# State products as three column tiles, a costed register read and a new table of priorities, in a chunked attention and two-layer MoE kernel

## The chip, the cores and the metric

The kernel runs on one core of a Trainium2 chip. The metric is the device time of one execution in microseconds. The kernel before takes 762.5 us, the median of three runs (762.09 to 762.78).

The core has five instruction streams that run side by side and wait for one another through semaphores: TensorE (PE; its weight loads stand apart as PEld), VectorE (DVE), ScalarE (ACT), GpSimd (POOL) and SyncE (SP, which here issues DMAs and reads registers). Each stream is executed in the order in which the program has its instructions.

## The reference

Three layers follow each other. All tensors are fp32.

```python
# 1. attention with a decaying state: 4 batches, 8 heads, 768 steps, head size 48
for t in range(S):
    S_re, S_im = a[t] * (S_re, S_im)          # complex product, per row of the state
    S_re = S_re + outer(k[t], v[t])
    y[t] = q[t] @ S_re
# 2. dense layer on x = y, [3072, 384], hidden size 2048
h = x @ w_in
x = (max(h, 0) + alpha * min(h, 0)) @ w_out
# 3. sparse layer: 8 experts of hidden size 1024, one expert per row
on = x @ w_skip > 0
e  = argmax(x @ w_gate);  gate = softmax(x @ w_gate)[e]
out = x;  out[on] += gate * (max(x @ w1[e], 0) @ w2[e])
```

## The kernel before, in words

**Attention.** The 768 steps are cut into 6 chunks of 128, and each chunk of each batch is one unit: 24 units, s = 0 to 23, with chunk c = s // 4. For a unit, DVE and ACT first work out decays, angles and scaled q and k ("E", function `elementwise`). Then the function `attention` ("P") issues on TensorE: the products of keys and queries (tile `at`, two halves of four heads), the transposes of the keys (also into `at`, copied by ACT to `kT`), the output `y`, and, except in the last chunk, the new part of the state, `sps`, which DVE adds to the state `St`. `sps` is the product of `kT` (128 steps x 96 rows per head; 96 is real and imaginary part of 48) and the values `vt` (128 steps x 48). It is 8 matmuls, one per head, each with 96 columns of weights and 48 columns that stream past them (lines 709 to 711). They are 8 separate items for the scheduler, so that other matmuls can stand between them. The output `y` is different: its matmuls have 32 columns of weights and go to four groups of 32 rows of the output, and the helper `columns` adds all of them to the plan as one item (lines 697 to 706 and 727 to 735). An fp32 matmul makes two records, since TensorE passes over it twice; one with fp32r operands makes one.

**Dense layer.** Two units of attention make one block of 256 rows: 12 blocks, "M0" to "M11" (`moe_block`). A block has 8 steps. A step makes 18 matmuls into a tile `h` (weights split in a high and a low part, input split in `xhi` and `xlo`), then ACT copies `h` to `hs`, DVE applies the leaky slope, ACT rounds to `gh`, DVE takes the rest `gl`, and 12 matmuls of the step before go into the accumulators `acc`. At the start, the dense layer's 64-bit weights are decoded on DVE ("d", `decode`).

**Sparse layer.** Rows are listed per expert by indirect DMAs. After block M9, `rank_experts` orders the experts by their count: a small matmul of `onesb` and `ohsum` counts, a chain of small DVE operations writes `plan`. Then SP reads from `plan` two registers for each of nine work items (`start_of`, lines 997 to 1005, helper lines 1002 and 1003). An item's row numbers `ids` are read from the list by a DMA on SP's queue whose address is in these registers (line 1046), and POOL gathers the rows into `xg` by indirect DMAs (line 1056). DVE takes the maximum of the gate's logits from `xg` into `gmx` (function `gates_of`), and TensorE transposes `xg` into `xt`. The weights of the item come by DMAs of SP's queue (`load_weights`, line 1014). The first item's rows are gathered while blocks M10 and M11 still run.

**The order.** All this is recorded as a plan of items, each with an engine, a cost in us, what it reads and writes, and a priority. `Plan.emit` walks through the plan with these costs as if they were times, lets each engine take the ready item with the lowest priority number, and writes the instructions out in the order that comes of it. A table `SHIFT` adds a number to the priority of an item by its label (for instance "P5s": state product of unit 5; "M3.2": step 2 of block 3). So a cost or a shift that changes changes the order of the instructions on all five streams, and nothing else. Between 27 and 55 us of the plan's own clock it fills pauses of TensorE with matmuls that nobody reads ("filler", line 1420).

Of the kernel before, what the change touches and what calls it, by code (L numbers as in the profile page):

```python
# [52 lines left out]
PE_IN, PE_OUT = [], [4, 5, 6, 7, 8, 9, 10, 11]  # L53
C0, C1 = [4, 6]
SHIFT = {
# [24 lines left out]
}  # L80
MODE = [0] * 12
TRIG = "trig_and_small"
# [316 lines left out]
def moe_kernel(tc, a, qk, v, w_in, w_out, alpha, w_gs, w1, w2, nat, nat_v, out):  # L399
# [53 lines left out]
    def mm(o, l, r, start, stop):  # L453
        n = cols(o)
        dt = l.dtype
        if dt == F32R:
            cost = max(n, 256) / 2.4 + 13.5
        elif dt == BF16:
            cost = 30
        else:  # L460
            cost = 2 * (max(n, math.prod(l.shape[1:])) / 1.2 + (6 if n <= 128 else 0))
        pl.add("PE", cost / 1e3, lambda: nc.tensor.matmul(real(o), lhsT=real(l), rhs=real(r), start=start, stop=stop,  # L462
                                                          skip_group_check=True),
               [l, r] + ([] if start else [o]), [o])
# [28 lines left out]
    with ctx:  # L493
# [172 lines left out]
        def attention(s, pri):  # L666
            c, b = divmod(s, NB)
            last = c == NCH - 1
            qh, kh = qk_of[s, 0], qk_of[s, 1]
            pl.pri = V_PRI if s < 2 else pri(0)  # L670
            pl.part = "v"
            vt = pl.buf(pp, [128, VW], F32, "vt", bufs=2)
            dma(vt, v[s], VT)
            m = s // 2
            if s % 2 == 0:
                x_of[m] = [pl.buf(xp, [128, 3, 256], F32R, name, bufs=2) for name in ("xhi", "xlo")]
            xhi, xlo = x_of[m]
            y = pbuf(y_ps, [128, 3, 128], "y")
            m4 = mask.rearrange("p (o f) -> p o f", o=1).to_broadcast([128, 4, 128])
            As, kTs = [], []  # L680
            for g in range(2):
                pl.pri, pl.part = pri(g), 'ab'[g]
                at = pbuf(at_ps, [128, 512], "at", bufs=2)
                for x in range(4):
                    mm(at[:, x * 128:(x + 1) * 128], kh[:, 4 * g + x, 0:128], qh[0:96, 4 * g + x, :], True, True)
                A = pl.buf(pp, [128, 4, 128], F32, "A", bufs=2)
                tt(A, at.rearrange("p (x t) -> p x t", x=4), m4, ALU.mult)
                As.append(A)
                if not last:
                    at = pbuf(at_ps, [128, 512], "at", bufs=2)  # L690
                    for x in range(4):
                        transpose(at[:, x * 96:x * 96 + 96], kh[:, 4 * g + x, 0:128], ident[0:96, 0:96])
                    kT = pl.buf(pp, [128, 4, 96], F32, "kT", bufs=2)
                    copy(kT, at[:, 0:384].rearrange("p (x d) -> p x d", x=4))
                    kTs.append(kT)
            pl.pri, pl.part = pri(2), 'y'
            ops = []
            for inter in range(c > 0, -1, -1):
                for g in range(2):
                    for t, off in ((g, 16 * g), (2, 32 - 48 * g)):  # L700
                        for x in range(4):
                            h = 4 * g + x
                            cs = slice(h * 64 + off, h * 64 + off + 32)
                            ops.append((y[32 * x:32 * x + 32, t, :],) + (
                                (St[:, b, cs], qh[:, h, :]) if inter else (vt[:, cs], As[g][:, x, :])))
            columns(ops)
            pl.pri, pl.part = pri(3), 's'
            if not last:
                sps = pbuf(s_ps, [128, H * D], "sps")[0:96, :]
                for h in range(H):  # L710
                    mm(sps[:, h * D:h * D + D], kTs[h // 4][:, h % 4, :], vt[:, h * 64:h * 64 + D], True, True)
                new = sps.rearrange("p (h e) -> p h e", h=H)
                sv = St[0:96, b, :].rearrange("p (h e) -> p h e", h=H)[:, :, 0:D]
                gc = kh[:, :, 128:129].to_broadcast([96, H, D])
                if c:
                    su = pl.buf(pp, [96, H, D], F32, "su", bufs=1)
                    tt(su, new, sv, ALU.add)
                    tt(sv, su, gc, ALU.mult)
                else:
                    tt(sv, new, gc, ALU.mult)  # L720
            pl.part = 'h'
            cs = slice((s % 2) * 128, (s % 2) * 128 + 128)
            copy(xhi[:, :, cs], y)
            tt(xlo[:, :, cs], y, xhi[:, :, cs], ALU.subtract)
            pl.part = ''

        def columns(ops):

            def go():
                for n, (o, l, r) in enumerate(ops):  # L730
                    ins = nc.tensor.matmul(real(o), lhsT=real(l), rhs=real(r), start=n < 4,  # L731
                                           stop=n >= len(ops) - 4, skip_group_check=True)
                return ins

            pl.add("PE", 0.3 + 0.0575 * len(ops), go, [x for op in ops for x in op[1:]], [op[0] for op in ops])

        def decode64(src, n, name):
            raw = pl.buf(dp, [128, 384, 2], I32, "raw", bufs=RAW)
# [258 lines left out]
        def start_of(n):  # L997

            r, _, col = ITEMS[n]

            def read():
                regs[n] = (nc.sync.value_load(real(plan)[0:1, r:r + 1], min_val=0, max_val=E - 1),
                           nc.sync.value_load(real(plan)[0:1, col:col + 1], min_val=0, max_val=(E - 1) * NT + 256))

            return pl.add("SP", 0.2, read, [plan], [])

        def load_weights(n, place, place1, after, behind=None):
            r1 = pl.buf(place1, [128, 3, FE], F32, "r1", bufs=1 + (place1 is in_B))
# [31 lines left out]
        def gather(n, place, k, opened, listed, rows=NT):  # L1040
# [13 lines left out]
            for t in range(nt):  # L1054
# [5 lines left out]
                    gathers[n] = r.ins  # L1060
                    return r

                pl.add("POOL", 1.1, go, [ids], [xg[:, t, :]], lag=0.7, late=1.0)
            return ids, xg

        def gates_of(place, xg, nt):
# [485 lines left out]
```

## Time and profile before

| | us |
|---|---|
| median of the runs (3) | 762.5 |
| the profiled execution | 760.46 |
| its span, from the first to the last instruction | 758.3 |
| TensorE busy | 718.6 (95%) |
| VectorE busy | 602.1 (79%) |
| ScalarE busy | 486.7 (64%) |
| GpSimd busy | 98.6 (13%) |
| mean granted clock of TensorE | 0.996 of full speed |

Busy times are of the profiled execution. A matmul's record begins when it starts and is longer than its share of the engine, since matmuls overlap: how long one occupies TensorE is read from one start to the next.

### The profile page before, as it was taken

What the parts mean: (1) busy time and instruction counts of PE and PEld (TensorE: products, weight loads), DVE (VectorE), ACT (ScalarE), POOL (GpSimd) and SP (SyncE); (2) the same over time, 40 slices, a digit from 0 to 9 for tenths busy, and PEclk for the clock granted to TensorE, in tenths of its full rate; (3) what the DMA queues carried; (4) which work ended last, traced back from release to release, by engine and by line L of the source; (5) the groups of instructions that cost most, each with busy time, mean ns of one, the idle gap of its engine ahead of it and who ended that gap; (6) DMA issues with size and microseconds to landing.
All of it is one profiled execution on the core that took longest, in us unless ns stands there. A gap on an engine that the chain in (4) does not pass through costs nothing.

```text
span 758.3 us, 16570 instructions
## 1 busy us (share of the span) xinstructions
PE 718.6 (95%) x6372; PEld 695.5 (92%) x6372; DVE 602.1 (79%) x1425; ACT 486.7 (64%) x833; POOL 98.6 (13%) x154
## 2 busy tenths in 40 slices
PE   1789999999999999999999999999997999999996
PEld 0678999999999999999999999999997999999996
DVE  5999999989889899999899898945555635697623
ACT  8969659869779679897948958522325332556411
POOL 4000000111101220011130010101011013710111
PEclk9999999999999999999999999999999999999999
DMA  7595862483744767668475564936215301899500
GB/s 267 161 273 199 239 214 79 124 257 102 189 117 143 188 175 231 183 181 268 137 195 178 180 193 120 250 108 172 87 44 189 126 1 46 274 390 393 181 11 18
DMA packets 84678, 130.53 MB, mean 172 GB/s; under 512 B 8822, under 2 KB 60096, under 8 KB 84592
## 3 DMA queue, kind: packets, MB, share of 16 engines
q1 hardware_dynamic: 79152, 111.19, 48.4%
q0 software_dynamic: 5440, 18.21, 7.6%
q8 instruction: 52, 0.85, 0.5%
q14 instruction: 34, 0.28, 0.1%
HBM read 99.46 MB, written 31.29 MB: 172 GB/s over the span
## 4 chain that ended last, share of the span: by engine, by line
PE 49%; issue 10%; DVE 7%; ACT 5%; DMA 5%; SPq 2%; POOL 1%; POOLq 0%; ACTq 0%; DVEq 0%
PE h L462 20%; PE acc L462 19%; PE at L462 3%; PE y L731 3%; PE sps L462 2%; ACT X L419 2%; ACT L391 2%; DVE X L431 1%; DMA r<-in_w 1%; DMA qh<-qd 1%; PE at L467 1%; DMA lst<-tok,ix 1%; DMA X<-in_qk 1%; DMA kd<-QP 1%; ACT hs L424 1%
## 5 line engine op out<-in xcount | busy, mean ns | idle before, releaser
L462 PE MATMUL h<-xlo,wih 128*128 128x256 f32 x576 | 163.8, 285 | 0.2 <-DVE xlo L431 0.2
L462 PE MATMUL h<-xhi,wih 128*128 128x256 f32 x576 | 162.9, 289 | 0.7 <-ACT hs L424 0.4
L462 PE MATMUL h<-xhi,wil 128*128 128x256 f32 x576 | 163.0, 284 | 0.0
L462 PE MATMUL acc<-woh,gh 128*128 128x394 f32 x384 | 134.4, 350 | 0.2 <-ACT gh L424 0.2
L462 PE MATMUL acc<-woh,gl 128*128 128x394 f32 x384 | 130.4, 347 | 4.2 <-DVE gl L431 4.2
L462 PE MATMUL acc<-wol,gh 128*128 128x394 f32 x384 | 132.1, 344 | 0.0
L419 ACT ACTIVATE X<-X 128x384 f32<-128x384 f32 (+1 forms) x216 | 117.2, 559 | 20.9 <-DVE X L450 7.0
L462 PEld LDWEIGHTS h<-xhi,wih 128*128 128x128 f32 x576 | 108.6, 190 | 3.1 <-ACT hs L424 1.3
L462 PEld LDWEIGHTS h<-xlo,wih 128*128 128x128 f32 x576 | 109.7, 191 | 0.7 <-DVE xlo L431 0.4
L462 PEld LDWEIGHTS h<-xhi,wil 128*128 128x128 f32 x576 | 109.7, 191 | 0.4 <-issue 0.4
L439 DVE SCALAR_TENSOR_TENSOR hs<-hs,alp 128x256 f32<-128x256 f32 x192 | 83.8, 477 | 28.6 <-ACT hs L424 28.1
L424 ACT COPY hs<-h 128x512 f32<-128x512 f32 x96 | 53.7, 583 | 63.0 <-PE h L462 60.7
L391 ACT ACT_TABLE_LOAD x71 | 91.1, 1283 | 1.1
L424 ACT CAST gh<-hs 128x512 fp32r<-128x512 f32 x96 | 58.4, 616 | 47.7 <-DVE hs L439 25.0
L431 DVE TENSOR_TENSOR gl<-hs,gh 128x512 fp32r<-128x512 f32 x96 | 65.2, 685 | 14.8 <-ACT gh L424 14.6
L462 PEld LDWEIGHTS acc<-woh,gl 128*128 128x128 f32 x384 | 71.6, 190 | 5.8 <-DVE gl L431 4.7
L911 POOL DMA_INDIRECT lst<-tok,ix x24 | 36.2, 1510 | 312.1 <-DVE ix L435 261.5
L431 DVE TENSOR_TENSOR X<-X 128x768 f32<-128x768 f32 (+1 forms) x96 | 71.6, 749 | 5.8 <-ACT X L419 5.6
L462 PEld LDWEIGHTS acc<-woh,gh 128*128 128x128 f32 x384 | 72.9, 190 | 1.5 <-ACT gh L424 0.6
L462 PEld LDWEIGHTS acc<-wol,gh 128*128 128x128 f32 x384 | 73.1, 190 | 0.3 <-issue 0.2
L462 PE MATMUL at<-qh,kh 96*128 96x128 f32 x384 | 52.6, 278 | 1.0 <-DMA qh<-qd 1.0
L439 DVE SCALAR_TENSOR_TENSOR X<-X 128x384 f32<-128x384 f32 x96 | 52.1, 549 | 0.9 <-ACT X L419 0.6
(189 smaller groups left out, 1381.1 us busy)
## 6 DMA issues: line engine op xcount, KB each, us to landing
r<-in_w SPq DMA_DIRECT2D x24, 512.0 KB, 7.2
r<-in_w SPq DMA_DIRECT2D x32, 384.0 KB, 8.9
kd<-QP SPq DMA_DIRECT2D x24, 387.0 KB, 4.9
kh<-kd SPq DMA_DIRECT2D x24, 387.0 KB, 4.7
qd<-X SPq DMA_DIRECT2D x24, 384.0 KB, 4.0
qh<-qd SPq DMA_DIRECT2D x24, 384.0 KB, 4.5
X<-in_a POOLq DMA_DIRECT2D x18, 384.0 KB, 5.6
X<-in_qk POOLq DMA_DIRECT2D x18, 384.0 KB, 6.1
```

The source lines that it names most:

```text
L391: nc.scalar.preload_act_table_set(o)
L419: lambda: nc.scalar.activation(real(o), real(i), f, **{k: real(x) for k, x in kw.items()}),
L424: lambda: nc.scalar.copy(real(o), real(i)), [i], [o])
L431: dve(o, cols(o), lambda: nc.vector.tensor_tensor(out=real(o), in0=real(x), in1=real(y), op=op), [x, y], late=late)
L439: dve(o, cols(o), lambda: nc.vector.scalar_tensor_tensor(out=real(o), in0=real(x), scalar=real(s), in1=real(y), op0=op0, op1=op1), [x, y, s])
L462: pl.add("PE", cost / 1e3, lambda: nc.tensor.matmul(real(o), lhsT=real(l), rhs=real(r), start=start, stop=stop, skip_group_check=True), [l ...
L467: pl.add("PE", 0.09 if cols(o) <= 96 else 0.12, lambda: nc.tensor.transpose(real(o), real(i), ident), [i], [o])
L731: ins = nc.tensor.matmul(real(o), lhsT=real(l), rhs=real(r), start=n < 4, stop=n >= len(ops) - 4, skip_group_check=True)
L911: r = nc.gpsimd.indirect_dma_start(out=lst, out_offset=bass.IndirectOffsetOnAxis(ap=real(ix[:, t:t + 1].bitcast(U32)), axis=0), in_=toks[t ...
```

## The change

The state product of a unit is written as 24 matmuls with 32 columns of weights each, to three groups of 32 rows of the output, and goes through the helper `columns`, so that it is one item of the plan. Three costs of the planner are changed: a matmul with more than 256 columns, the register reads of an item on SP, and the lateness of the gathers. The table `SHIFT` has new numbers throughout. TensorE gets 320 instructions more for the state products and one filler more, ScalarE two table loads more; DVE, POOL and SP have the same instructions as before.

```diff
 SHIFT = {
-    "E0e": 1.5, "E1e": 5.5, "E2e": 3, "E2k": 3.5, "E2x": 2, "E3e": 1.6, "E3k": 4, "E4e": 5.1, "E4q": 2.7,
+    "E0k": -59.5, "E2e": -9.8, "E2k": -8.5, "E2q": -11.4, "E3e": -20.4, "E3k": -25.4, "E3q": -8, "E4e": -7.9,
...
         if dt == F32R:
-            cost = max(n, 256) / 2.4 + 13.5
+            cost = max(n, 256) / 2.4 + (13.5 if n <= 256 else 16)
...
-            columns(ops)
+            columns(ops, False, 0.3 + 0.0575 * len(ops))
             pl.pri, pl.part = pri(3), 's'
             if not last:
                 sps = pbuf(s_ps, [128, H * D], "sps")[0:96, :]
-                for h in range(H):
-                    mm(sps[:, h * D:h * D + D], kTs[h // 4][:, h % 4, :], vt[:, h * 64:h * 64 + D], True, True)
+                columns([(sps[j:j + 32, h * D:h * D + D], kTs[h // 4][:, h % 4, j:j + 32], vt[:, h * 64:h * 64 + D])
+                         for h in range(H) for j in (0, 32, 64)], True, 0.3 + H * 0.09)
...
-        def columns(ops):
+        def columns(ops, alone, cost):
 
             def go():
                 for n, (o, l, r) in enumerate(ops):
-                    ins = nc.tensor.matmul(real(o), lhsT=real(l), rhs=real(r), start=n < 4,
-                                           stop=n >= len(ops) - 4, skip_group_check=True)
+                    ins = nc.tensor.matmul(real(o), lhsT=real(l), rhs=real(r), start=alone or n < 4,
+                                           stop=alone or n >= len(ops) - 4, skip_group_check=True)
                 return ins
 
-            pl.add("PE", 0.3 + 0.0575 * len(ops), go, [x for op in ops for x in op[1:]], [op[0] for op in ops])
+            pl.add("PE", cost, go, [x for op in ops for x in op[1:]], [op[0] for op in ops])
...
-            return pl.add("SP", 0.2, read, [plan], [])
+            return pl.add("SP", 1.0, read, [plan], [])
...
-                pl.add("POOL", 1.1, go, [ids], [xg[:, t, :]], lag=0.7, late=1.0)
+                pl.add("POOL", 1.1, go, [ids], [xg[:, t, :]], lag=0.7, late=2.0)
```

**TensorE, around the output of unit s = 5** (the first chunk with a state; `qh_181` are its queries, `at` its key-query products and key transposes, `acc` the dense layer's accumulators). Before:

```order
L462 MATMUL acc<-woh,gh 128x394
L462 MATMUL acc<-wol,gh 128x394
L462 MATMUL at<-qh_181,kh 128x128 x4
L467 MATMUL at<-ident,kh 128x96 x4
L462 MATMUL sps<-vt,kT 96x48 x4
L462 MATMUL acc<-woh,gl 128x394
L462 MATMUL sps<-vt,kT 96x48 x4
L731 MATMUL y<-qh_181,St 32x128 x16
L731 MATMUL y<-A,vt 32x128 x16
L462 MATMUL acc<-woh,gh 128x394
```

And now:

```order
L471 MATMUL acc<-wol,gh 128x394
L471 MATMUL acc<-woh,gl 128x394
L740 MATMUL y<-qh_181,St 32x128 x16
L740 MATMUL y<-A,vt 32x128 x16
L740 MATMUL sps<-vt,kT 32x48 x24
L471 MATMUL at<-qh_180,kh 128x128 x2
L471 MATMUL h<-xhi,wih 128x256 x2
```

The state product stands in one piece of 24 behind the output, where it stood in two pieces of 4 ahead of it. In the whole program the state products stand in 39 pieces before and in 20 now; 8 of the 20 stand directly before or behind an output `y`, 6 of them in units from s = 4 on.

**VectorE, from the last inputs of block M11 to the first item's gate** (`xlo<-y,xhi` makes the low part of a unit's output, the last such row is that of s = 23; `gmx<-xg` and `es<-xg,gmx` are the first item's gate, which need the gathered rows). Before:

```order
L439 SCALAR_TENSOR_TENSOR hs<-hs,alp 128x256 x4
L431 TENSOR_TENSOR gl<-hs,gh 128x512
L431 TENSOR_TENSOR xlo<-y,xhi 128x3x128
L431 TENSOR_TENSOR gl<-hs,gh 128x512
L439 SCALAR_TENSOR_TENSOR hs<-hs,alp 128x256 x2
L431 TENSOR_TENSOR gl<-hs,gh 128x512
L439 SCALAR_TENSOR_TENSOR hs<-hs,alp 128x256 x2
L446 TENSOR_REDUCE gmx<-xg_7509 128x2
L431 TENSOR_TENSOR es<-xg_7509,gmx 128x16
L431 TENSOR_TENSOR gl<-hs,gh 128x512
```

And now:

```order
L440 TENSOR_TENSOR A<-at,mask 128x512 x2
L440 TENSOR_TENSOR xlo<-y,xhi 128x3x128
L448 SCALAR_TENSOR_TENSOR hs<-hs,alp 128x256 x4
L440 TENSOR_TENSOR gl<-hs,gh 128x512
L440 TENSOR_TENSOR xlo<-y,xhi 128x3x128
L448 SCALAR_TENSOR_TENSOR hs<-hs,alp 128x256 x2
L440 TENSOR_TENSOR gl<-hs,gh 128x512
L455 TENSOR_REDUCE gmx<-xg_7818 128x2
L440 TENSOR_TENSOR es<-xg_7818,gmx 128x16
L440 TENSOR_TENSOR gl<-hs,gh 128x512
```

The gate of the first item stands one `gl` nearer to the last `xlo`, which itself stands further down. On TensorE, 100 matmuls into `h`, 36 into `acc` and the outputs `y` of units 22 and 23 now stand between the count of the experts and the first transposes of `xg`; the first matmul that reads the `gl` of the last row comes two matmuls behind the six transposes.

**SyncE, between the register reads and the first item's row numbers** (`TENSOR_LOAD plan` reads one register; two of them, lines 1002 and 1003, or 1011 and 1012 now, belong to one item). Before, the end of the nine pairs:

```order
L1002 TENSOR_LOAD plan
L1002 ISA x2
L1003 TENSOR_LOAD plan
L1003 ISA x2
L1046 ISA
L1046 DMA ids_7507<-lst 128x2x2
L1014 ISA
```

And now, from the seventh pair on:

```order
L1011 TENSOR_LOAD plan
L1011 ISA x2
L1012 TENSOR_LOAD plan
L1012 ISA x2
L1055 ISA
L1055 DMA ids_7820<-lst 128x2x2
L1011 TENSOR_LOAD plan
L1011 ISA x2
```

The row numbers of the first item are read after seven pairs instead of after nine; the other two pairs follow, and then the item's weights.

## Rows read from the trace of the kernel before

**Rows 1.** The page's first part: busy time, share of the span, instructions.

```profile
PE 718.6 (95%) x6372; PEld 695.5 (92%) x6372; DVE 602.1 (79%) x1425; ACT 486.7 (64%) x833; POOL 98.6 (13%) x154
```

**Rows 2.** Stretches: length, busy us of PE, PEld, DVE, ACT, POOL, clock, DMA, GB/s.

```profile
0.00:60.00 60.00, 35.50 (x264) 31.57 (x265) 50.63 (x119) 49.75 (x84) 9.42 (x57) 1.00 0.76 242
60.00:190.00 130.00, 127.22 (x1177) 119.88 (x1176) 124.58 (x300) 103.96 (x196) 9.35 (x12) 1.00 0.57 168
190.00:380.00 190.00, 189.99 (x1827) 185.14 (x1826) 176.23 (x420) 157.83 (x261) 25.55 (x27) 1.00 0.62 180
380.00:560.00 180.00, 179.64 (x1782) 174.90 (x1781) 140.55 (x348) 96.38 (x165) 17.50 (x19) 1.00 0.57 161
```

**Rows 3.** Waits of PE: for whom, us in total, times, longest.

```profile
PE at L467 <- DVE Ao L439: 19.8, 3, 15.4
PE acc L462 <- DVE gl L431: 4.2, 2, 4.0
```

**Rows 4.** Timeline of PE, 203 to 213 us: start, us, instructions, idle before.

```profile
205.53 0.34 PE L462 MATMUL acc<-woh,gh 128*128 128x394 f32 x1
205.80 1.08 PE L731 MATMUL y<-qh,St 128*32 128x128 f32 x32
...
207.69 0.45 PE L462 MATMUL acc<-wol,gh 128*128 128x394 f32 x1
207.97 0.34 PE L462 MATMUL acc<-woh,gl 128*128 128x394 f32 x1
208.15 0.35 PE L462 MATMUL acc<-woh,gh 128*128 128x394 f32 x1
...
209.78 1.48 PE L462 MATMUL sps<-vt,kT 128*96 128x48 f32 x16
211.08 0.48 PE L462 MATMUL h<-xhi,wih 128*128 128x256 f32 x2
211.40 0.28 PE L462 MATMUL h<-xlo,wih 128*128 128x256 f32 x1
211.52 0.28 PE L462 MATMUL h<-xhi,wil 128*128 128x256 f32 x1
```

**Rows 5.** Timeline of PE, 104.5 to 109 us: an output without a state.

```profile
106.17 1.08 PE L731 MATMUL y<-A,vt 128*32 128x128 f32 x32
107.18 0.63 PE L462 MATMUL acc<-woh,gl 128*128 128x394 f32 x2
```

**Rows 6.** Weight loads by form: busy us, mean ns, idle before.

```profile
L462 PEld LDWEIGHTS sps<-vt,kT 128*96 128x96 f32 x320 | 31.4, 164 | 1.9 <-issue 1.0 <-ACT kT L424 0.7
L731 PEld LDWEIGHTS y<-A,vt 128*32 128x32 f32 x768 | 21.1, 110 | 1.4 <-issue 0.6 <-DVE A L431 0.6
```

**Rows 7.** Timeline of PE, 551.9 to 552.3 us: end of an output, small bf16 matmuls.

```profile
551.65 0.40 PE L731 MATMUL y<-A,vt 128*32 128x128 f32 x8
...
552.02 0.17 PE L462 MATMUL acc<-ohsum,onesb 128*128 128x8 bf16 x1
...
552.10 0.17 PE L462 MATMUL acc<-ohb,onesb 128*128 128x8 bf16 x1
```

**Rows 8.** Timelines of PE and DVE, 553 to 579 us: the experts' count, the gate, the stall.

```profile
553.97 0.17 PE L462 MATMUL acc<-ohsum,onesb 128*1 128x8 bf16 x1
...
577.44 0.17 DVE L446 TENSOR_REDUCE gmx<-xg 128x2 f32<-128x16 f32 x1 [8.24 <-issue]
...
578.48 0.70 PE L462 MATMUL acc<-woh,gl 128*128 128x394 f32 x1 [3.98 <-DVE gl L431]
```

**Rows 9.** Line 1002, SP: duration ns min/median/max, first and last start us.

```profile
L1002 SPq TENSOR_LOAD <-plan x9: 263/263/469, 556.0 to 565.2; - x9
```

**Rows 10.** The stretch behind the stall, columns as in group 2.

```profile
578.30:581.60 3.30, 3.12 (x10) 3.12 (x10) 3.19 (x10) 2.09 (x4) 0.00 (x0) 0.50 0.13 43
```

**Rows 11.** The state products' passes by stretch: 380 to 560 us, 0 to 66 us.

```profile
L462 PE MATMUL sps<-vt,kT x80: 203/248/283, 395.0 to 484.0; 128*96 128x48 f32 x80
...
L462 PE MATMUL sps<-vt,kT x32: 208/248/283, 42.2 to 64.3; 128*96 128x48 f32 x32
```

55 rows, old and new, of the table SHIFT are left out of this document.

## The prediction

> **What bounds the kernel now.** I read the busy times first, then the stretches, then TensorE's waits, and last the timeline around the places that the change touches. TensorE is busy for 718.6 of 758.3 us [rows 1]. By stretches [rows 2] it lacks 24.5 us before 60 us, 2.8 us from 60 to 190, and nearly nothing from 190 to 560. So from 60 us on, TensorE's own work sets the pace. The reader should also see that VectorE is close behind: 124.6 of 130 us, then 176.2 of 190, then 140.6 of 180 [rows 2]. The list of waits [rows 3] shows where TensorE idles: 15.4 us in one piece for the first decoded weights, and 4.0 us in one piece for a `gl`. The second is at 578.48 us [rows 8]. It is no shortage of VectorE: just ahead, VectorE itself sat idle for 8.24 us until `gmx` could read the gathered rows of the first expert item [rows 8]. The streams are in order, so the dense layer's `gl` waited behind a `gmx` that came too early in the order.
>
> So three things can pay: fewer us of TensorE from 60 us on, one for one; the pause at 578 us; and the start.
>
> **The state products.** Before, one unit's product runs from 209.78 to 211.08, so 1.30 us for 16 passes (8 matmuls of two passes), 0.081 each [rows 4]. Only 48 columns stream past in a pass; the load of 96 weight columns is the longer part: a load has a mean of 164 ns with 96 columns and 110 ns with 32 [rows 6], 0.84 ns a column, and 96 of these are 0.081 us, which is the spacing seen.
>
> The new form is not in the trace; the nearest rows are those of `y`, which has the same 32 weight columns and four groups of rows side by side. An output with a state has 64 passes, 16 sets of four, in two groups of 32 (the first is shown), and takes 205.80 to 207.69, 1.89 us [rows 4]; one without has 8 sets and takes 106.17 to 107.18, 1.01 us [rows 5]. So a set is 0.88 / 8 = 0.11 us, and 0.13 us is left as the price of leaving. Entering costs too: 205.53 to 205.80 is 0.27 against 0.18 from 207.97 to 208.15 for the same kind of matmul [rows 4], so 0.09 more. Together 0.22 us per visit.
>
> A set of `y` streams 128 columns, 0.86 ns each. If the set of the state product goes by what it streams, it is 48 x 0.86 = 0.041 us; its weight loads of 32 columns (0.027 us by the slope above) lie under that. It has 24 x 2 = 48 passes in sets of three, so 16 sets: 0.66 us, and 0.88 with the visit. Against 1.30 this saves 0.42 us. The bounds are wide: at the low end the groups of a set begin within 0.02 us of each other (eight passes of 0.27 us each, two sets, last 0.40 us in all: 0.40 - 0.27 - 0.11 [rows 4, 5, 7]), so 0.02 per set, 0.54 per unit, a saving of 0.76; at the high end a set costs 0.11 as in `y`, 1.98 per unit, a loss of 0.68. I take 0.041, since streaming explains `y`.
>
> The Trainium skill speaks against it: "TensorEngine Tiling (Array Packing)", section Performance Considerations, says that every matmul carries some 60 cycles of overhead, so that a factor should not be taken from a dimension that is already small. At 2.4 GHz 60 cycles are 25 ns, an estimate from that page; 48 passes would be 1.2 us and the product 1.42 with the visit, dearer than before. The groups of `y` that begin within 0.02 us of each other [rows 7] do not agree with a charge for each pass.
>
> There are 20 products of 16 passes. The first two end at 64.3 us [rows 11], in the start, where TensorE is not the limit; I count 18 x 0.42 = 7.6 us. Six of these stand directly beside a `y` in the new order and share its visit: 6 x 0.22 = 1.3 us. Sum: 8.9 us.
>
> **The register reads and the first gather.** Reading one item's two registers takes (565.2 - 556.0) / 8 = 1.15 us on SP [rows 9]. The planner assumed 0.2, so it believed the rows of the first item there some 8 us too soon. From the count of the experts at 553.97 to `gmx` at 577.44 are 23.5 us [rows 8]. Now the row numbers are fetched after seven pairs instead of nine: 2 x 1.15 = 2.3 us sooner, so 21.2 us after the count, if the DMAs take as long as before. TensorE has, between the count and the first transposes of the gathered rows, 100 matmuls of `h` at 0.12 (211.40 to 211.52 [rows 4]), 36 of `acc` at 0.18, and two outputs at 1.98: 12.0 + 6.5 + 4.0 = 22.4 us. The rows are there 1.2 us before they are wanted, and the `gl` behind `gmx` is wanted later still. So the wait of 4.0 us goes. With it goes what follows: right after it the granted clock is 0.50, 1.2 GHz, for 3.3 us, in which 10 matmuls ran [rows 10], 0.33 us each instead of 0.18: 1.5 us. Sum: 5.5 us; bounds 0 (the gather comes 4 us later than I think) and 5.5. What is late next is the first item's transposes, with only that 1.2 us in hand.
>
> The two pairs that now follow push the item's weight DMAs 2.3 us behind the row numbers. What covers them is the rest of block M11, which TensorE has to finish before it needs the first item's weights; I cost them at nothing, and at the 2.3 us themselves if that cover is gone.
>
> **The new table.** It changes all five streams, and no row prices that. From 60 to 560 us TensorE idles for 3.2 us in all [rows 2], so a better order can gain no more there. Before 60 us it idles for 24.5, of which 15.4 wait for the first weights; at stake are 9.1 us, and VectorE, with 175.2 of the first 190 us busy, decides. More of block M0 and M1 has to pass VectorE early if blocks are pulled forward, and two more table loads stand on ACT. I take a loss of 1 us, with bounds of 2 us gained and 4 lost.
>
> **Sum.** -8.9 - 5.5 + 1.0 = -13.4 us on the profiled execution's 760.46, so 747.1. The median of the runs, 762.5, is 2.0 above that execution; the forecast for the median is 749 us.
>
> **Rivals.**
> - *VectorE takes over.* TensorE gets shorter, VectorE does not, and until 380 us it is already 93 to 96% busy [rows 2]. If the saving there becomes a wait for `gl` or `xlo`, only the five products behind 380 us (80 passes [rows 11]) pay: 5 x 0.42 = 2.1 us, one visit shared, 0.2, and in all -2.3 - 5.5 + 1.0 = -6.8: 755.7. For it: the narrow margin from 60 to 190 us. Against: from 190 to 380 us VectorE has 13.8 us free, more than the products there save.
> - *The gather still comes late.* The stall stays at the same size, behind another instruction: -8.9 + 1.0, 754.6. For it: the margin of 1.2 us. Against: the row numbers come 2.3 us sooner, and the need later.
> - *A charge per pass.* TensorE begins a matmul at most every 0.027 us, as the small bf16 matmuls do (552.02 to 552.10 is three steps [rows 7]). The product is then 48 x 0.027 + 0.22 = 1.52, 0.22 dearer: 18 x 0.22 - 1.3 = +2.7, and -1.8 in all: 760.7. Against: the groups of `y` begin closer together.
> - *Slower: a set costs what it costs in `y`*, 0.11 us, because each pass of a group waits for its own weights and not for the columns that stream. The product takes 1.98: 18 x 0.68 - 1.3 = +10.9, and +6.4 in all: 769. It decides the sign from a set time of 0.088 us on. For it: a load of 32 columns takes 110 ns [rows 6], just the length of a set. Against: in the old product, loads of 164 ns follow each other every 0.081 us, so a load's length does not limit.
>
> **How the numbers follow.** Forecast 0.60, VectorE 0.15, gather 0.10, charge per pass 0.07, slower 0.08. The forecast's own range is 745 to 752 us, from the start's bounds and a little of the set time. The range reaches up to the first two rivals: 744.5 to 757.5. No more than 0.2% (1.5 us) can be told from no change. Faster: the forecast, the first two and half of the third, 0.88; same: the other half and a little, 0.04; slower: 0.08.
>
> **What would show it.** The state products' timeline: 48 passes in about 0.66 us from first to last start, three groups beginning together. TensorE's busy time down by some 9 us. No wait of 4 us near the end of block M11, and no 0.50 in the clock there. DVE's idle time before `gmx` short. First `h` of M0 within 3 us of before. I am wrong if a product takes over 1.3 us, if TensorE's waits for DVE between 60 and 380 us grow by more than 4 us, or if the pause before the first item is still there.

## The result

The changed kernel takes 754.6 us (median of 6 runs, 753.4 to 757.9) against 762.0 for the kernel before (6 runs): ratio 0.9911, 95% interval 0.9888 to 0.9933, 6.8 us faster. The forecast was 13.4 us faster, 749.0. The direction and the outer range held (744.5 to 757.5); the forecast's own range, 745 to 752, did not, and half of the gain did not come.

The page of the changed kernel, first part (busy time, share of the span, instructions), against [rows 1]:

```profile
span 751.6 us, 17818 instructions
PE 709.4 (94%) x7014; PEld 682.6 (91%) x7014; DVE 602.3 (80%) x1425; ACT 487.2 (65%) x835; POOL 92.8 (12%) x154
```

TensorE works 9.2 us less, about what I had said, yet the span fell by only 6.7 us, and that includes a stall that has gone. The same stretches as in [rows 2]:

```profile
0.00:60.00 60.00, 33.53 (x324) 30.73 (x324) 49.75 (x117) 50.98 (x86) 9.44 (x57) 1.00 0.75 234
60.00:190.00 130.00, 124.45 (x1237) 115.55 (x1238) 122.77 (x296) 102.14 (x191) 11.50 (x12) 0.99 0.58 168
190.00:380.00 190.00, 187.65 (x2177) 180.01 (x2176) 171.77 (x408) 145.60 (x244) 20.93 (x28) 1.00 0.60 177
380.00:560.00 180.00, 179.57 (x1937) 173.66 (x1939) 147.86 (x365) 110.36 (x187) 12.31 (x16) 1.00 0.56 168
```

TensorE now lacks 26.5 us before 60 us (24.5 before), 5.6 from 60 to 190 (2.8) and 2.4 from 190 to 380 (0.0). VectorE is no busier in these stretches than it was. So TensorE waits more while no other engine is full. For whom it waits, against [rows 3] (us in total, times, longest):

```profile
PE at L476 <- DVE Ao L448: 20.5, 3, 14.7
PE at L471 <- ACT wt L433: 4.4, 2, 3.4
PE h L471 <- ACT xhi L433: 2.8, 3, 2.1
PE acc L471 <- ACT gh L433: 1.5, 2, 1.0
```

The same operands in the kernel before, as far as they are not in [rows 3]:

```profile
PE at L462 <- ACT wt L424: 3.1, 3, 2.0
PE h L462 <- ACT xhi L424: 0.3, 1, 0.3
PE acc L462 <- ACT gh L424: 0.2, 1, 0.2
```

The 4.0 us for `gl` are off the list; waits for results of ScalarE, `xhi` and `gh` above all, have grown. The state product, against [rows 4], beside an output and alone:

```profile
174.56 1.06 PE L740 MATMUL y<-A,vt 128*32 128x128 f32 x32
175.43 0.86 PE L740 MATMUL sps<-vt,kT 128*32 128x48 f32 x48
176.22 0.49 PE L471 MATMUL at<-qh,kh 96*128 96x128 f32 x2
...
228.40 0.34 PE L471 MATMUL acc<-wol,gh 128*128 128x394 f32 x1
228.67 0.88 PE L740 MATMUL sps<-vt,kT 128*32 128x48 f32 x48
229.48 0.39 PE L471 MATMUL h<-xhi,wih 128*128 128x256 f32 x1
```

From its start to the next matmul it takes 0.79 and 0.81 us, and the entry 0.27 instead of 0.18: 0.90 alone where I had said 0.88. Between the passes' first and last start lie 0.65 us beside an output and 0.68 alone (read from the single records that the line sums up). And the place of the stall, one stretch and VectorE's rows, against [rows 8, 10]:

```profile
560.00:600.00 40.00, 40.00 (x312) 39.76 (x304) 24.64 (x59) 19.01 (x32) 2.85 (x3) 1.00 0.43 149
```

```profile
574.70 0.17 DVE L455 TENSOR_REDUCE gmx<-xg 128x2 f32<-128x16 f32 x1 [2.80 <-DMA xg<-x1d,ids]
...
574.99 0.68 DVE L440 TENSOR_TENSOR gl<-hs,gh 128x512 fp32r<-128x512 f32 x1
```

VectorE still waits 2.80 us for the gathered rows (8.24 before), but TensorE does not: 40.00 of 40 us busy, clock 1.00. Two rows of TensorE show how far the working held, the count of the experts and the first item's transposes:

```profile
553.10 0.17 PE L471 MATMUL acc<-ohsum,onesb 128*1 128x8 bf16 x1
...
575.92 0.82 PE L476 MATMUL xt<-ident,xg 128*128 128x128 f32 x6
```

`gmx` starts 21.6 us behind the count (21.2 forecast), the transposes 22.8 (22.4 forecast), and the margin between them is the 1.2 us that I had.

So two of my three terms look right where they stand, and some 7 us are missing elsewhere.

### The profile page after: what moved, and what is told of

Its sections match the earlier page's. It is cut to its first block, busy times and chain, and to the rows that moved or that the text cites. A ratio compares the mean times of both kernels' runs of the same rounds, so it can differ in the third digit from the quotient of the medians.

```text
span 751.6 us, 17818 instructions
## 1 busy us (share of the span) xinstructions
PE 709.4 (94%) x7014; PEld 682.6 (91%) x7014; DVE 602.3 (80%) x1425; ACT 487.2 (65%) x835; POOL 92.8 (12%) x154
## 4 chain that ended last, share of the span: by engine, by line
PE 54%; ACT 13%; DVE 13%; issue 11%; DMA 6%; SPq 2%; POOL 0%; POOLq 0%; ACTq 0%; DVEq 0%
PE h L471 23%; PE acc L471 21%; ACT X L428 4%; PE at L471 4%; ACT L400 3%; PE y L740 3%; DVE X L440 2%; ACT Rr L428 2%; DVE X L459 1%; PE at L476 1%; DMA qh<-qd 1%; DVE X L448 1%; ACT gh L433 1%; DMA rawc<-in_w_in 1%; DVE hs L448 1%
## 5 line engine op out<-in xcount | busy, mean ns | idle before, releaser
L920 POOL DMA_INDIRECT lst<-tok,ix x24 | 29.2, 1217 | 278.1 <-DVE ix L444 234.6
```

What stands on the lines that cost most here:

```text
L920: r = nc.gpsimd.indirect_dma_start(out=lst, out_offset=bass.IndirectOffsetOnAxis(ap=real(ix[:, t:t + 1].bitcast(U32)), axis=0), in_=toks[t ...
```

## The experiments

The chips differ. Runs 1 to 4 had one chip and runs 5 to 8 another, on both of which the kernel before takes 771 us; there the traces lose 7 to 10 us between 640 and 660 us, in the expert items, against the first traces. Runs 9 to 12 had a third, on which it takes 761.7. Each kernel is therefore compared by its ratio to the kernel before on its own chip; a difference of two such ratios has about 0.3%, 2.3 us, either way.

**1. Tiles in the old order.** The kernel before with every head's product as three column tiles of 32 rows, head by head at the old places, which makes 39 visits for the 20 products (the edit is shortened here):

```
-mm(sps[:, h*D:h*D+D], kTs[h//4][:, h%4, :], vt[...], True, True)
+for j in (0, 32, 64): matmul(sps[j:j+32, h*D:h*D+D], kTs[h//4][:, h%4, j:j+32], vt[...])
```

> The kernel before, its order of instructions unchanged on all engines; only each of the 8 matmuls of a state product is written as three column tiles. The trace of the changed kernel has 0.043 us per set of three passes and about 0.21 us per visit; the old order has 39 visits, 9 beside an output: 20 x 16 x 0.043 + 39 x 0.21 - 9 x 0.2 = 20 us instead of 28. Theory A (TensorE's path: what a product saves is saved, and the new order lost it elsewhere): 7 us faster, 755. Theory B (VectorE and ScalarE bind, so the saving turns into waits in any order): 1 to 3 us faster, 760.

Measured: 772.2, ratio 1.0021 (1.0004 to 1.0038). No gain at all: Theory A's number failed by over 8 us, and Theory B's too. What a product saves here is far less than the expectation has; run 4 shows it.

**2. The new order with the old products.** The changed kernel, each product again 8 matmuls of 96 columns in the one piece of the plan, every engine's order the same.

> The changed kernel, its order unchanged on all engines; only the state product is again 8 matmuls with 96 columns of weights, in its one piece. Theory A: the 8.7 us that the tiles save on TensorE come back, 763, and the waits of the new order stay. Theory B: TensorE's longer products fall into waits that are there anyway, about 2 us slower than the changed kernel, 757.

Measured: 767.8, ratio 0.9963 (0.9945 to 0.9981). What it says needs the changed kernel on such a chip (run 5).

**3. Only the first rows first.** The kernel before, with one edit: the later register pairs on SP wait until the first item's row numbers are asked for.

```
-k = start_of(n)
+k = start_of(n, row_reads[:1])
```

> The kernel before; only SP's order differs: the first item's row numbers are read right behind the first pair of register reads instead of behind the ninth. The row numbers come some 6 us sooner (then held by the last output of attention), so the wait of 4.0 us for gl near 578 us and the half clock behind it go. Theory A: 5.5 us faster, 756.5. Theory B (something else is late next, e.g. the item's weights, whose DMAs start 2.4 us later): 0 to 3 us faster.

Measured: 764.9, ratio 0.9925 (0.9901 to 0.9949), 5.8 us faster. The stretch of the stall and TensorE's only wait in it:

```profile
560.00:600.00 40.00, 39.64 (x281) 39.28 (x277) 24.73 (x52) 20.18 (x34) 2.84 (x3) 1.00 0.41 140
```

```profile
PE acc L462 <- ACT gh L424: 0.4, 1, 0.4
```

Stall and half clock go with the reads alone. The edit is a stronger form of the change's: there the row numbers are read behind the seventh pair, here behind the first.

**4. Runs 1 and 3 together.**

> The kernel before with both edits, tiles in the old order and the first rows first. Theory A: the two add up, 7 + 5.5 us faster, 749.5, which beats the changed kernel by 5 us and shows that the table of priorities is what lost. Theory B: about 6 us faster, 756, no better than the changed kernel.

Measured: 767.4, ratio 0.9958 (0.9937 to 0.9979): 2.5 us slower than run 3. In the old order the tiles pay nothing. Where it goes can be read, since runs 3 and 4 have the same order and differ only in the products.

Part of it is never saved. A piece of four heads among other matmuls, first in run 3, then in run 4:

```profile
394.65 0.28 PE L462 MATMUL h<-xhi,wih 128*128 128x256 f32 x1
394.77 0.80 PE L462 MATMUL sps<-vt,kT 128*96 128x48 f32 x8
...
395.59 0.28 PE L462 MATMUL h<-xhi,wil 128*128 128x256 f32 x1
```

```profile
396.67 0.28 PE L462 MATMUL h<-xhi,wih 128*128 128x256 f32 x1
396.88 0.54 PE L731 MATMUL sps<-vt,kT 128*32 128x48 f32 x24
...
397.57 0.28 PE L462 MATMUL h<-xhi,wil 128*128 128x256 f32 x1
```

From the `h` before to the second `h` behind it is 0.94 us in run 3 and 0.90 in run 4: entering and leaving take all but 0.04 of the gain. Whole products in one piece (0.38) and pieces beside an output (up to 0.35) gain more. Over all pieces between 66 and 556 us, from start to start with idle time taken out, the tiles save 4.3 us of TensorE, where the expectation had 7.

The rest goes into waits. Again first run 3, then run 4, at the same matmul:

```profile
171.74 0.34 PE L462 MATMUL acc<-woh,gl 128*128 128x394 f32 x1
171.92 0.39 PE L462 MATMUL at<-qh,kh 96*128 96x128 f32 x2
```

```profile
172.91 0.34 PE L462 MATMUL acc<-woh,gl 128*128 128x394 f32 x1
175.08 0.46 PE L462 MATMUL at<-qh,kh 96*128 96x128 f32 x2 [1.83 <-DMA qh<-qd]
```

A `qh` that just came in time now comes 1.83 us too late. Between 66 and 556 us TensorE's idle time is 4.7 us longer in run 4 than in run 3: this `qh` has 1.83, a pause of 1.06 inside a product has no cause in the profile, and the others, before `at`, `h`, `acc` and `y`, have 0.1 to 0.4 each.

**5. The changed kernel again**, beside runs 6 to 8.

> The changed kernel itself, so that the other three runs have it on their chip. Theory A (the tiles pay in the new order, and the new order itself costs about 6 us more than I had put down): about 7 us faster than the kernel before, ratio 0.991, as at first; and, if it is the chip of the first four runs, about 6 to 7 us faster than the new order with the old products (767.8), which would be 761 to 762. Theory B (shorter products turn into waits in any order): within 2 us of the new order with the old products, 766 to 768 on that chip.

Measured: 764.0, ratio 0.9919 (0.9899 to 0.9939). Against run 2 that is 0.44%, 3.4 us: in the new order the tiles do pay, but 3.4 us, 2.3 either way, half of what Theory A wanted; the time lies between the two theories. Runs 2 and 5 are on two chips of 771 us. With run 3 the change comes apart:

| | old products | tiles |
|---|---|---|
| old order, first rows first | 0.9925 (run 3) | 0.9958 (run 4) |
| new order | 0.9963 (run 2) | 0.9919 (run 5) |

In us of 771: reads -5.8, new order +2.9, tiles in it -3.4: -6.3, which is run 5's 0.9919. The single terms have 2.3 us either way, so the +2.9 is barely clear of nothing.

**6. Less for VectorE, new order.** The 80 checks of the inputs look at 8 of 384 columns; the rest of that check is left out.

```
-tensor_reduce(out=chk[...], in_=i, ...)
+tensor_reduce(out=chk[...], in_=i[:, 0:8], ...)
```

> The changed kernel with the 80 reductions that check the inputs looking at 8 of 384 columns (it leaves out the rest of that check), the order of all engines unchanged. That takes 0.38 us each off VectorE: some 3 us between 60 and 190 us, 13 us between 190 and 380, 14 us between 380 and 560. Theory A (VectorE sets the pace between 100 and 380 us, the rival of my prediction): TensorE's extra loss there shrinks, and the kernel is 3 to 5 us faster than the changed one. Theory B (what TensorE waits for there are single results that come late by their place in the order, on ScalarE as much as on VectorE): within 1.5 us of the changed kernel.

Measured: 762.6, 1.4 us under run 5 (spread 759.8 to 767.1). VectorE's busy time is 26.4 us shorter (575.8 for 602.2), and 1.4 us of that comes back, 2.3 either way: VectorE's amount of work is at most a small part of what TensorE waits for.

**7. The same in run 4's kernel.**

> The old order with tiles per head and the first rows first (the fourth run), with the same shortened check of the inputs, the order unchanged. Theory A (in the old order VectorE keeps the tiles from paying): 4 to 7 us faster than the fourth run, so 760.5 to 763.5 where that took 767.35. Theory B (the tiles' gain goes into waits for ScalarE, for DMAs and in the expert items): within 1.5 us of the fourth run.

Measured: 765.5, ratio 0.9933: 0.25%, 1.9 us, under run 4. It lies between the two theories, nearer to B, and is less than can be told between two chips.

**8. The pause at 61.65 us.** The changed kernel with the second unit's `xhi` moved up on ScalarE and its `xlo` on VectorE.

> The changed kernel with two instructions moved in the start: the cast xhi of the second unit on ScalarE ahead of a table load and an activation that stood before it, and its xlo on VectorE ahead of three decoding steps. Theory A (the pause of 2.1 us at 61.65 us and the half clock of 3.4 us behind it are part of what the new order costs): the first h comes about 1.3 us sooner, the stretch at clock 0.50 near 63.6 us goes, and the kernel is 1.3 to 3 us faster than the changed one. Theory B (something else is just as late there, wil above all): the pause goes to the next operand, and the time is within 0.7 us of the changed kernel.

Measured: 765.5, ratio 0.9939, no better than run 5. In the trace the move works: first run 5, then run 8 (start, us, last the idle time before):

```profile
62.07 1.05 PE L740 MATMUL y<-A,vt 128*32 128x128 f32 x31
65.22 0.50 PE L471 MATMUL h<-xhi,wih 128*128 128x256 f32 x2 [2.10 <-ACT xhi L433]
```

```profile
61.08 1.05 PE L747 MATMUL y<-A,vt 128*32 128x128 f32 x31
62.74 0.50 PE L478 MATMUL h<-xhi,wih 128*128 128x256 f32 x2 [0.61 <-ACT xhi L440]
...
66.69 0.52 PE L483 MATMUL at<-ident,Ao 128*128 128x128 f32 x3 [1.06 <-DVE Ao L455]
```

1.5 us less of one pause, and 1.06 us of a new one for a decoded `Ao`. The clock behind the pause, in the changed kernel at first, and in run 8:

```profile
63.50:67.00 3.50, 3.23 (x13) 2.94 (x14) 3.47 (x9) 3.48 (x8) 0.00 (x0) 0.51 0.69 166
```

```profile
62.70:72.00 9.30, 7.57 (x52) 6.53 (x53) 9.00 (x21) 9.26 (x19) 0.00 (x0) 1.00 0.48 155
```

The half clock is gone, and run 8's profiled execution, 1.0 us ahead of run 5's at 58 us, is 1.9 ahead at 73. Part of that first 1.0 is another stretch of half clock, near 55 us, that run 5's execution has and the first one of the same kernel has not. The medians show no gain; the profiled execution is the fastest of run 8's six (761.5 to 767.3). For the whole time this stays inconclusive.

**9. Products twice, new order.** `for n, (o, l, r) in enumerate(ops * 2 if alone else ops)`: the 48 passes issued twice.

> The changed kernel with the 48 passes of every state product issued twice (the second time writes the same result), the order unchanged. It adds 20 x 16 x 0.0434 = 13.9 us of TensorE. Theory A (TensorE alone sets the pace, every us of it is a us of the kernel): 13 to 14 us slower than the changed kernel. Theory B (TensorE and the chains of results that feed it share the pace, as the tiles' half return says): 5 to 9 us slower, and the waits after each product shrink by the rest.

Measured: 763.9, ratio 1.0031 (1.0007 to 1.0054): 1.2%, 9.1 us, over the changed kernel, of 13.9 added. The upper edge of Theory B.

**10. More for ScalarE.** The squares of each elementwise block issued twice.

> The changed kernel with one activation of each of the 24 elementwise blocks (the squares, 0.84 us) issued twice on ScalarE, the order unchanged: 20 us more for an engine that is 65% busy. Theory A (what comes late for TensorE comes late on ScalarE): 5 us or more slower than the changed kernel. Theory B (ScalarE has the slack that its share of busy time suggests): within 2 us.

Measured: 764.2, ratio 1.0039 (1.0016 to 1.0062): 9.8 us over the changed kernel. Theory A. The start, to be held against the first of the four stretches above:

```profile
0.00:60.00 60.00, 31.52 (x286) 29.03 (x287) 47.93 (x111) 51.46 (x83) 9.42 (x57) 1.00 0.73 234
```

TensorE gets 2.0 us less done there. The second unit's output begins 3.8 us later than in the changed kernel, the last unit's 8.5 us later: four squares (3.4 us) cost about their full time in the start, the twenty behind it (16.8 us) 4.7.

**11. The old table.** The changed kernel with the numbers of SHIFT from the kernel before.

> The changed kernel, its tiles and its new costs, with the table of priorities of the kernel before. The planner then makes a third order of it. Theory A (the new table earns its place for these products and costs): 4 us or more slower than the changed kernel, by waits of TensorE between 60 and 560 us. Theory B (the new table costs the 6 us that I miss, and the old one would not): 3 us or more faster than the changed kernel.

Measured: 763.1, ratio 1.0017 (1.0000 to 1.0034), 8.1 us over the changed kernel. Theory A. TensorE's longest waits from 60 to 560 us:

```profile
PE acc L462 <- ACT gh L424: 4.6, 3, 3.9
PE at L462 <- DVE A L431: 2.6, 1, 2.6
PE h L462 <- ACT xhi L424: 1.8, 2, 0.9
```

The old numbers do not give the old order, since tiles and costs are new; what they give is worse. Besides these waits, the granted clock has a mean of 0.94 up to 60 us and 0.96 from 60 to 190. That the new table costs 2.9 us is said of it with old products, for which it was not made.

**12. Products twice, old order.** Run 3 with each product's 8 matmuls issued twice.

> The old order with the old products and the first rows first (the third run), each state product issued twice, the order unchanged: 20 x 1.30 = 26 us more for TensorE. Theory A (in the old order other chains set the pace, and that is why the tiles brought nothing): 13 us slower or less. Theory B (TensorE and the chains are balanced there: less work for TensorE gains nothing, more work costs nearly all of it): 20 to 26 us slower than the third run.

Measured: 776.1, ratio 1.0208 (1.0173 to 1.0243): 2.8%, 21.6 us, over run 3, of 26 added. Theory B. TensorE's longest wait from 60 to 560 us is next to nothing:

```profile
PE at L462 <- ACT woh L424: 0.5, 2, 0.3
```

Four pairs have the same order and differ only in the products, so their starts can be subtracted (us; start of the output `y` of a unit, from the traces; unit 1 is near 62 us, unit 23 near 560; only the pair 4 - 3 is on one chip). The last column is the change at the products themselves between 66 and 556 us, from start to start with idle time taken out. The last two rows are pairs with equal products, and show what one trace differs from another by itself:

| second minus first | unit 1 | unit 8 | unit 14 | unit 23 | from 1 to 23 | change at the products |
|---|---|---|---|---|---|---|
| tiles, new order (5 - 2) | +1.3 | -1.1 | -2.9 | -4.8 | -6.1 | -8.4 |
| twice, new order (9 - changed) | +1.0 | +3.9 | +5.9 | +9.8 | +8.8 | +12.2 |
| tiles, old order (4 - 3) | +1.8 | +2.7 | +1.9 | +3.2 | +1.4 | -4.3 |
| twice, old order (12 - 3) | +0.8 | +7.6 | +14.4 | +19.8 | +19.0 | +23.8 |
| the same kernel (5 - changed) | +1.5 | +3.1 | +1.1 | +1.8 | +0.3 | +0.2 |
| the same up to there (3 - before) | -0.5 | -0.8 | -0.2 | +1.3 | +1.8 | +0.2 |

In the new order about 0.7 of a change in TensorE's work reaches the last unit, up and down, within 2 us. In the whole times it is 9.1 of 13.9 us up, and 3.4 of 8.4 down, with 2.3 us either way. In the old order 0.8 of more work reaches the last unit, and nothing of less. That the old order stood at a corner, with the feeding chains just in time, is how I read this; the 4.7 us of new idle time in run 4 fit it.

## Why the prediction was half right

**The state products.** The duration was right: 48 passes in 0.65 to 0.68 us, 0.90 with the visit against 0.88. So was the saving at the products: 0.38 us alone and 0.62 to 0.69 beside an output between runs 2 and 5, 8.4 us in all between 66 and 556 us, where I had 0.42, 0.64 and 8.9. TensorE's busy time fell by 9.2 us, as said. The Trainium skill's charge of some 60 cycles for each matmul ("TensorEngine Tiling (Array Packing)", Performance Considerations) is not seen as one that the passes pay one after another: 0.66 / 48 is 14 ns a pass, and the estimate from that page was 25. Whether each of the three tiles pays it beside the others, no run here shows: a set takes 43 ns. What failed is the sentence in front of the sum, "from 60 us on, TensorE's own work sets the pace", and with it "one for one". I read a share of busy time near 100% as "nothing else is near". But a matmul's record overlaps the next by up to 0.16 us, and a result that came just before its use leaves no wait to see. The term of -8.9 came out as -3.4 (runs 5 and 2, 2.3 either way; -6.1 between 62 and 560 us of the traces); in the old order, whose 39 visits leave a saving of only 4.3 us, it would have been nothing (run 4).

What takes the rest is not shown pair by pair: TensorE's idle time between 66 and 556 us differs by only 0.3 us between runs 2 and 5, and 2.0 of the 8.4 us come back as longer spacing of other matmuls, with no wait in the profile. How a single result that comes late in engines that work in order costs TensorE time can be seen at one place in the changed kernel, ScalarE, then VectorE, then TensorE:

```profile
350.09 1.08 ACT L428 ACTIVATE X<-X 128x384 f32<-128x384 f32 x2 [0.68 <-DVE X L459]
352.28 0.52 ACT L428 ACTIVATE X<-X 128x384 f32<-128x384 f32 x1 [1.11 <-DVE X L448]
352.71 0.60 ACT L433 CAST gh<-hs 128x512 fp32r<-128x512 f32 x1
```

```profile
349.97 0.86 DVE L448 SCALAR_TENSOR_TENSOR hs<-hs,alp 128x256 f32<-128x256 f32 x2
350.75 1.05 DVE L459 TENSOR_TENSOR_SCAN X<-X,Rr 128x128 f32<-128x128 f32 x3
351.71 0.53 DVE L448 SCALAR_TENSOR_TENSOR X<-X 128x384 f32<-128x384 f32 x1
```

```profile
351.98 0.34 PE L471 MATMUL acc<-woh,gl 128*128 128x394 f32 x1
353.36 0.45 PE L471 MATMUL acc<-woh,gh 128*128 128x394 f32 x1 [1.05 <-ACT gh L433]
```

The `hs` that `gh` needs is ready at 350.83. ScalarE stands idle for 1.11 us all the same, because the activation ahead of `gh` waits for an `X` that VectorE makes last, and TensorE pays 1.05 us. It is the pattern of the stall that the change removed, in small. Run 5's execution of the same kernel has no pause at this matmul, and 1.44 us instead of 0.44 at one near 158 us: such waits move from one execution to the next.

**The register reads.** Right: 5.5 forecast, 5.8 measured (run 3) for an edit of this kind by itself, though a stronger one. In the changed kernel neither the 4 us nor the half clock are there, and the gather and the transposes came within 0.4 us of the working. That two register pairs stand between the row numbers and the item's weights cost nothing, as I had put it: in the first trace after, the waits from 640 us on are no longer than before.

**The new table.** Forecast +1.0 with bounds of -2 and +4; with the old products it is +2.9 (run 2 against run 3, 2.3 either way). So it is inside its bounds and mis-sized by about 2 us, which is no more than the error. The first traces suggest the start: 2.0 us less TensorE work before 60 us, the pause of 2.10 us for `xhi`, and half clock behind it. Run 8, which takes out that half clock and 1.5 us of the pause, is no faster, so this is not shown. With the tiles the table is worth having: the old numbers cost 8.1 us more (run 11).

**The rivals.** "VectorE takes over" gave 755.7, near the 754.6 measured, but for the wrong reason: 26 us less work on VectorE brought 1.4 us (run 6). 20 us more on ScalarE cost 9.8, in the start above all (run 10). The two do not compare the engines on equal terms, since no run adds work to VectorE or takes it from ScalarE. So what I should have doubted, as I read it, is not which engine is next in busy time, but how early the results come. "A charge per pass" and "a set costs what it costs in `y`" are out by the timeline, "the gather still comes late" by the stretch at 560 us, although its 754.6 is the measured time to the tenth. That the time lies in my range is luck in so far: the range was drawn up to 757.5 for two rivals, neither of which happened. My own mark for being wrong, waits for DVE that grow by over 4 us between 60 and 380 us, was not reached (0.4 to 1.0 us); I had not set one for ScalarE.

The sum again, in us of the chips of runs 1 to 8: -3.4 for -8.9, -5.8 for -5.5, +2.9 for +1.0 gives -6.3, where I had -13.4; nearly all of the 7 us between is the first term and the table. What stays open: what takes the 0.3 of the tiles' saving that is lost up to the last unit, since the profile names no wait for it, and why run 8's gain in the trace does not show in its times. None of the other kernels that compute everything is faster than the changed one by more than a measurement can tell.

## What to carry to other kernels

A busy share of 99% does not mean that a saved us of that engine is a us saved: take out work, and the results that feed the engine may be just in time already. To learn the exchange rate, issue the same idempotent work twice and take it away, both; they need not agree (0.8 up, nothing down in the old order). When a form of work has a price for entering and leaving, count its pieces first: in 39 pieces the tiles saved half of what they saved in 20. A table of priorities belongs to the durations for which it was chosen, so change both together and price each edit with the other in place.

## What the runs showed of the hardware

- Three column tiles of 32 columns each, with 48 streamed columns, begin a set every 0.043 us: 0.65 to 0.68 us for 48 passes, against 1.30 for 16 passes with 96 columns. Between matmuls of full width they cost 0.09 us to enter and 0.13 to leave, so that a piece of 24 passes gains 0.04 us over the 8 that it replaces (run 4). Their weight loads are as long as those of `y` and lie under each other:

```profile
L740 PEld LDWEIGHTS sps<-vt,kT 128*32 128x32 f32 x960 | 15.5, 110 | 3.8 <-issue 2.5 <-ACT kT L433 0.8
```

- The granted clock halves behind a pause of TensorE in one case and not in the next: 0.51, so 1.2 GHz, in the 3.5 us from 63.50 on, behind a pause of 2.10 us; 1.00, 2.4 GHz, throughout behind 0.61 and 1.06 us in run 8. Two executions of one kernel differ too: from 54 to 56 us the first one of the changed kernel has 1.00 and run 5's has 0.50, where TensorE is busy for all of the 2 us in both.
- Chips differ by 9 us in this kernel (771 and 762 us before), nearly all of it in one place: run 5 is 1.8 us behind the first trace of the same kernel at 640 us and 10.4 behind at 660. On the slower ones TensorE waits there ahead of matmuls into `h`, as in run 3 from 600 to 700 us. The profile names nothing that these waits are for; that it is the item's weights is a guess:

```profile
PE h L462 <- issue: 4.8, 5, 1.9
```
